# One four-bank PSUM tile for sixteen heads' attention logits, one Exp over it, and reordered first loads, in a four-layer kernel

## The chip, the core and the metric

The kernel runs on one core of a Trainium2 chip. Its engines are TensorE (PE; weight loads are shown apart as PEld), VectorE (DVE), ScalarE (ACT), GpSimd (POOL) and SyncE (SP, which here only issues DMAs). The metric is the device time of one execution in microseconds (us), the median of several runs; less is better. The profile is a hardware trace of one execution.

## The reference

Four layers in a row, each added to its input: attention (A), gated mixer (B), A, B, with the same weights both times. S = 2048 tokens, D = 576, 32 heads of 18 elements. Attention looks back over 8 keys, two tokens apart:

```python
def _A_ref(x, wqkv, wo):                  # H=32, Dh=18, W=8, dil=2
    qkv = (x @ wqkv).reshape(B, S, 3, H, Dh)            # -> q, k, v per head
    idx = pos[:, None] - off[None, :]     # off = 0, 2, ..., 14
    mask = idx >= 0
    kg = k[:, :, idx_c, :]; vg = v[:, :, idx_c, :]      # gathered keys and values
    logits = einsum('bhsd,bhswd->bhsw', q, kg) * Dh ** -0.5
    logits = where(mask, logits, -1e9)
    o = einsum('bhsw,bhswd->bhsd', softmax(logits), vg)
    return o.reshape(B, S, D) @ wo

def _B_ref(x, w_in, w_sp, b_sp, w_out):   # F = 4608, Fh = 2304
    z = gelu(x @ w_in); z1 = z[..., :Fh]; z2 = layernorm(z[..., Fh:])
    g = einsum('ts,bsf->btf', w_sp, z2) + b_sp[None, :, None]
    return (z1 * g) @ w_out

x = x + A(layernorm(x)); x = x + B(layernorm(x))
x = x + A(layernorm(x)); x = x + B(layernorm(x))
```

## The kernel before

All matmul operands are bf16. Each A layer projects q and k in column blocks (`PG`, 512 tokens and 128 columns at a time, for q and k), copies them to a staging tile, and moves them by DMA to one place per head: tile `QK` holds four heads in each group of 128 partitions, 32 partitions a head, of which 18 hold the head and 14 hold fixed window rows. These rows add a large negative number to every logit outside the window, so that a dense 128-key by 112-query product with a plain Exp computes the windowed softmax. The window rows come from a small pattern built on GpSimd and VectorE, written to DRAM (`win_period`) and loaded again (`win_pat`).

The attention loop then runs over 19 token tiles t of 112 queries, twice each for 16 heads (step s, 38 in a layer): logits `L_mm`, Exp `EXP`, values `PV` with the row sums in an extra column of ones. The logits of step s+1 are issued ahead of the values of step s; further work of the layer (late projections `PG`, values `VW`, output projection `WO`, layer norm) is hung into the steps by a table.

```python
def H_tile(self, name):                    # 2 PSUM banks, two of them
    return self.ps.tile([P, 2, 512], f32, name=name, tag="H", bufs=2)
def PT_tile(self, shape, dt, name):        # 1 PSUM bank, four of them
    return self.ps.tile(shape, dt, name=name, tag="PT", bufs=4)
...
def L_mm(s):
    t, hf = divmod(s, 2)
    nk, nq = tdim(t)
    L_tiles[s] = [self.H_tile("L_ps") for _ in range(2)]
    for jp in range(2):
        for ftl in range(4):
            g = 4 * hf + ftl
            for jj in range(2):
                j = 2 * jp + jj            # the group of 32 rows
                nc.tensor.matmul(L_tiles[s][jp][:nk, jj, ftl * QT:ftl * QT + nq],   # line 426
                                 lhsT=kT[32 * j:32 * j + 32, g, QT * t:QT * t + nk],
                                 rhs=qT[32 * j:32 * j + 32, g, QT * t + PADL:QT * t + PADL + nq],
                                 start=True, stop=True, tile_position=(32 * j, 0))
def EXP(s):                                # line 435, two instructions a step
    for jp, L_ps in enumerate(L_tiles.pop(s)):
        Lv = L_ps[:, :, 0:4 * QT].rearrange("p a (b c) -> p a b c", c=QT)
        nc.scalar.activation(out=P_bufs[(2 * s + jp) % 4][:nk, :, :, 0:nq], in_=Lv[:nk, :, :, 0:nq],
                             func=ACT.Exp, scale=scale)
...
L_mm(0); EXP(0)
for d, qk, cc in pre:                      # six more projections
    PG(d, qk, cc, True, q2)
for s in range(NST):
    if s + 1 < NST:
        L_mm(s + 1); EXP(s + 1)
    PV(s)
    for f, a in table.pop(s, []):
        f(*a)
```

The start of the first layer (cut): the first loads go out on two queues, the normalised x of tiles 0 to 3 is transposed on TensorE (`T_pe`, copied to `xnT` by ScalarE), that of the other tiles by DMA on SyncE's queue (`T_`).

```python
x_load(x0[:, 0:2, :], 0, 2, nc.sync); x_load(x0[:, 2:4, :], 2, 2, nc.sync)
self.load_wv(nc.scalar)
x_load(x1[:, 0:4, :], 4, 4, nc.sync)
self.load_wqk(nc.sync)
self.zero_right(); exp_table()
self.build_window_rows(sb, nc.scalar)      # ends with a DMA from ScalarE's queue: win_period
nc.scalar.copy(out=v_ext[:, :, :, DH:DH + 1], in_=self.ones[...])      # line 517
self.make_ident(); setup_bufs(nc.gpsimd)
x_load(spare, 8, 4, nc.sync)
self.load_pat(nc.sync)                     # win_pat <- win_period
for _ in range(28):                        # warming matmuls, result unused
    nc.tensor.matmul(warm[:, 0:P], lhsT=self.ident[:], rhs=self.ident[:], start=True, stop=True)
S_(0, 1); E_(0, 2); R_(0, 2); S_(2); A_(0, 1); T_pe(0); T_pe(1)   # statistics, power on GpSimd, normalise
VW(0, ...); VW(1, ...); ...; T_pe(2); T_pe(3); ...; VW(2, ...)
... A_(4, 5); T_(4, 5); ... A_(6, 7); T_(6, 7)
self.fill_window_rows(QK, 0)
for k_, (d, cc) in enumerate(order):       # (0..2, block 0), (0..2, block 1), (3, 0), (3, 1), (4, 0), (4, 1)
    for qk in ((1, 0) if d < 4 else (0,)):
        PG(d, qk, cc, False, (nc.gpsimd, nc.sync) if d in (0, 4) else (nc.gpsimd, nc.gpsimd, nc.sync))
    if k_ == 3: R_(8, 4); A_(8, 9, 10, 11); T_(8, 9, 10, 11); S_(12, 13, 14, 15); E_(12, 4)
    if k_ == 5: self.fill_window_rows(QK, 1); R_(12, 4); A_(12, 13, 14, 15)
T_(12, 13, 14, 15)
for t in range(3, 8): VW(t, ...)           # then the loop above
```

The last argument of `PG` is the list of queues over which its eight moves into `QK` are dealt in turn. The mixer layers use the same H tiles for their first product and the same PT tiles for the gate and the output.

Of the kernel before, what the change touches and what calls it, by code (L numbers as in the profile page):

```python
# [9 lines left out]
ACT = mybir.ActivationFunctionType  # L10
# [8 lines left out]
P = 128  # L19
# [43 lines left out]
class K:  # L63
# [24 lines left out]
    def setup(self):  # L88
        nc, tc, cfg, ctx = self.nc, self.tc, self.cfg, self.ctx
        S = cfg.S  # L90
        self.consts = ctx.enter_context(tc.tile_pool(name="consts", bufs=1))
        self.dram = ctx.enter_context(tc.tile_pool(name="dram", bufs=1, space=DRAM))
        c = self.consts
        self.neg_half = c.tile([P, 1], f32, name="neg_half")
        nc.vector.memset(self.neg_half[:], -0.5)
        self.eps_t = c.tile([P, 1], f32, name="eps_t")
        nc.vector.memset(self.eps_t[:], EPS)
        self.xnT = c.tile([P, 5, cfg.XW], bf16, name="xnT")
        nc.gpsimd.memset(self.xnT[:, :, 0:PADL], 0.0)

        self.ident = c.tile([P, P], bf16, name="ident")
        self.ones = c.tile([P, 1], bf16, name="ones")
        nc.vector.memset(self.ones[:], 1.0)
        nl = len(cfg.layers)
        self.xres = [self.dram.tile([S, D], f32, name=f"xres{i}") for i in range(nl - 1)]
        self.ps = ctx.enter_context(tc.tile_pool(name="ps", bufs=1, space=PSUM))
        self.right = None
        self.bridge = ctx.enter_context(tc.tile_pool(name="bridge", bufs=1))
        xb = self.bridge.tile([P, 4 * 640], bf16, name="ln_xn")
        self.bsp = xb[:, 0:cfg.S]  # L110
        self.xn_bufs = [xb[:, i * 640:(i + 1) * 640] for i in range(4)]
        self.xn_rr = 0
        self.deferred = []

    def build_window_rows(self, c, eng):
# [31 lines left out]
        nc.vector.tensor_scalar(out=n[:], in0=n[:], scalar1=15, scalar2=None, op0=ALU.bitwise_and)  # L147
        nc.vector.tensor_scalar(out=g[:], in0=n[:], scalar1=1, scalar2=None, op0=ALU.logical_shift_right)
        nc.vector.tensor_tensor(out=g[:], in0=g[:], in1=n[:], op=ALU.bitwise_xor)
        for i in range(4):  # L150
            nc.vector.tensor_scalar(out=bits[:, i, :], in0=g[:], scalar1=i, scalar2=1,
                                    op0=ALU.logical_shift_right, op1=ALU.bitwise_and)
        nc.vector.tensor_scalar(out=bits[:, 4, :], in0=n[:], scalar1=1, scalar2=None, op0=ALU.bitwise_and)
        nc.vector.tensor_scalar(out=vf[:], in0=bits[:], scalar1=-2.0, scalar2=1.0, op0=ALU.mult, op1=ALU.add)
        nc.vector.tensor_scalar_mul(out=R[:, :, 0:8, :], in0=R[:, :, 0:8, :], scalar1=vf[:, 4, 1:2])
        nc.vector.tensor_tensor(out=uu[:], in0=vf[:, 0:4, 0:2], in1=vf[:, 0:4, 1:3], op=ALU.add)
        nc.vector.tensor_scalar_mul(out=R[:, 0, 8:12, :], in0=vf[:, 0:4, 1:2].to_broadcast([P, 4, 16]), scalar1=half)
        nc.vector.tensor_scalar_mul(out=R[:, 1, 8:12, 0:2], in0=uu[:, :, 0:1].to_broadcast([P, 4, 2]), scalar1=0.5)
        nc.vector.tensor_scalar_mul(out=R[:, 1, 8:12, 2:16], in0=uu[:, :, 1:2].to_broadcast([P, 4, 14]), scalar1=0.5)
        one = self.dram.tile([2, MR, 256], bf16, name="win_period")  # L160
# [5 lines left out]
        self.dma(one[:].rearrange("a r (p f) -> p (a r) f", f=16), R[0:16].rearrange("p a r f -> p (a r) f"), eng=eng)  # L166
# [4 lines left out]
        self.load_pat = load  # L171

    def make_ident(self):
        nc = self.nc
        for xb in self.xn_bufs:
            nc.gpsimd.memset(xb[:, D:640], 0.0)
        nc.gpsimd.memset(self.ident[:], 0.0)
        nc.gpsimd.affine_select(out=self.ident[:], in_=self.ident[:], compare_op=ALU.not_equal, fill=1.0,
                                base=0, pattern=[[-1, P]], channel_multiplier=1)
# [12 lines left out]

    def H_tile(self, name):
        return self.ps.tile([P, 2, 512], f32, name=name, tag="H", bufs=2)
# [118 lines left out]
    def layer_A(self, li):  # L313
# [14 lines left out]
        P_bufs = [main.tile([P, 2, 4, P], bf16, name=f"P_sb{k_}") for k_ in range(4)]  # L328
# [9 lines left out]
        if li == 0:  # L338
            w2 = R["win2a"][:].rearrange("p c n -> p (c n)")
            lent = [w2[:, k_ * 2 * CBW:(k_ + 1) * 2 * CBW].rearrange("p (a b) -> p a b", a=2) for k_ in range(2)]  # L340
        man = tc.manual_schedule(engines={ET.PE, ET.Activation, ET.DVE, ET.Pool, ET.SP})
# [73 lines left out]
        L_tiles = {}  # L415

        def L_mm(s):
            t, hf = divmod(s, 2)
            nk, nq = tdim(t)
            L_tiles[s] = [self.H_tile("L_ps") for _ in range(2)]  # L420
            for jp in range(2):
                for ftl in range(4):
                    g = 4 * hf + ftl
                    for jj in range(2):
                        j = 2 * jp + jj
                        nc.tensor.matmul(L_tiles[s][jp][:nk, jj, ftl * QT:ftl * QT + nq],  # L426
                                         lhsT=kT[32 * j:32 * j + 32, g, QT * t:QT * t + nk],
                                         rhs=qT[32 * j:32 * j + 32, g, QT * t + PADL:QT * t + PADL + nq],
                                         start=True, stop=True, tile_position=(32 * j, 0))

        def EXP(s):
            nk, nq = tdim(s // 2)
            for jp, L_ps in enumerate(L_tiles.pop(s)):
                Lv = L_ps[:, :, 0:4 * QT].rearrange("p a (b c) -> p a b c", c=QT)
                nc.scalar.activation(out=P_bufs[(2 * s + jp) % 4][:nk, :, :, 0:nq], in_=Lv[:nk, :, :, 0:nq], func=ACT.Exp,  # L435
                                     scale=scale)

        def PV(s):
            t, hf = divmod(s, 2)
            nk, nq = tdim(t)  # L440
            O_ps = self.PT_tile([P, 512], f32, "O_ps")
            for jp in range(2):
                for ftl in range(4):
                    for jj in range(2):
                        idx = 4 * ftl + 2 * jp + jj
                        nc.tensor.matmul(O_ps[:, idx * (DH + 1):(idx + 1) * (DH + 1)],  # L446
                                         lhsT=P_bufs[(2 * s + jp) % 4][:nk, jj, ftl, :],
                                         rhs=v_ext[:nk, t, 16 * hf + idx, :], start=True, stop=True)
            Ov = O_ps[:, 0:16 * (DH + 1)].rearrange("p (h e) -> p h e", e=DH + 1)
            o_t = o_bufs[t % len(o_bufs)]  # L450
            rec = sb.tile([P, 16], f32, name="rec", tag="rec", bufs=2)
            nc.vector.reciprocal(out=rec[:nq, :], in_=Ov[:nq, :, DH])
            nc.vector.tensor_tensor(out=o_t[:nq, 288 * hf:288 * (hf + 1)].rearrange("p (h d) -> p h d", d=DH),
                                    in0=Ov[:nq, :, 0:DH], in1=rec[:nq, :, None].to_broadcast([nq, 16, DH]), op=ALU.mult)
            if hf == 1:
                c0 = (QT * t) % (RING * P)
                if t < NT - 2:
                    nc.sync.dma_start_transpose(out=oT[:, :, c0:c0 + nq], in_=o_t[:nq, :])
# [38 lines left out]


        if li == 0:
# [11 lines left out]
            self.load_wv(nc.scalar)  # L511
            x_load(x1[:, 0:4, :], 4, 4, nc.sync)
            self.load_wqk(nc.sync)
            self.zero_right()
            exp_table()
            self.build_window_rows(sb, nc.scalar)
            nc.scalar.copy(out=v_ext[:, :, :, DH:DH + 1], in_=self.ones[:, None, None, :].to_broadcast([P, NT, H, 1]))
            self.make_ident()
            setup_bufs(nc.gpsimd)
            x_load(spare, 8, 4, nc.sync)  # L520
            self.load_pat(nc.sync)
            warm = self.PT_tile([P, 512], f32, "warm")
            for _ in range(28):
                nc.tensor.matmul(warm[:, 0:P], lhsT=self.ident[:], rhs=self.ident[:], start=True, stop=True)
# [39 lines left out]
            S_(2)  # L564
# [5 lines left out]
            S_(3)  # L570
            E_(2, 2)
            R_(2, 2)
            VW(1, 0, False)
            VW(1, 1, False)
            S_(4)
# [3 lines left out]
            S_(5)  # L579
# [17 lines left out]
            for k_, (d, cc) in enumerate(order):  # L597
                for qk in ((1, 0) if d < 4 else (0,)):
                    PG(d, qk, cc, False, (nc.gpsimd, nc.sync) if d in (0, 4) else (nc.gpsimd, nc.gpsimd, nc.sync))
# [6 lines left out]
                if k_ == 5:  # L606
                    self.fill_window_rows(QK, 1)
                    R_(12, 4)
                    A_(12, 13, 14, 15)
            T_(12, 13, 14, 15)  # L610
            nvw0, nvw = 3, 8
# [14 lines left out]
        q2 = (nc.gpsimd, nc.sync, nc.gpsimd)  # L626
# [65 lines left out]
    def layer_B(self, li):  # L692
# [7 lines left out]

        zu_cm = pool("zu")
# [257 lines left out]
def build_kernel(ctx, tc, aps, cfg):  # L959
# [7 lines left out]
    k.run_deferred()  # L967

# [53 lines left out]
```

The softmax here doesn't subtract the row's maximum and nothing guards it: scores larger than these inputs give would overflow.

## Time and profile before

| | |
|---|---|
| median time, 3 runs | 1202.52 us (1201.88 to 1202.58) |
| span of the profiled execution | 1199.5 us, 20636 instructions |
| granted TensorE clock, mean | 0.999 |
| attention layers | about 0 to 145 us and 610 to 731 us |
| logits (line 426) | 1216 matmuls 32x112, median 208 ns each |
| Exp (line 435) | 152 instructions, 126.7 us, mean 916 ns for the full shape 128x896 |
| values (line 446) | 1216 matmuls 128x19, median 171 ns each |
| first v projection starts | 12.22 us |
| first q and k projection starts | 18.47 us |

In the profile's views each row is a group of equal instructions in order of time: start, length, engine, line of the kernel, operation, output <- inputs, shape, count, and in brackets the idle time of the engine before it and what ended it. "ACTq", "SPq" are the queues of the engines that issue DMAs. The duration of a matmul runs until its result is written, so that matmuls overlap one another: sixteen of 208 ns can lie within 0.40 us. A weight load may lie beside a matmul.

### The profile page before, as it was taken

To read this page: it belongs to the slowest core of one execution; us is meant where nothing else is said; L and a number is where in the kernel's file an instruction comes from. 1 tells how busy PE (TensorE), PEld (TensorE's weight loads), DVE (VectorE), ACT (ScalarE), POOL (GpSimd) and SP (SyncE) were. 2 spreads that over 40 slices of the span, in tenths; PEclk is the share of its full clock that TensorE was granted. 3 is DMA by queue.
4 is the path that set the end of the run, shared out by engine and by line. 5 is a ranking of instruction groups with operands and counts; after the bars stand their busy time and mean duration, and the time that the engine had idled before them with its cause. 6 is when DMAs were issued, how large, how long until landed. Compare 5 with 4: busy or idle time off the path is not lost.

```text
span 1199.5 us, 20636 instructions
## 1 busy us (share of the span) xinstructions
PE 1173.9 (98%) x8438; PEld 620.1 (52%) x8536; DVE 544.7 (45%) x1199; ACT 377.9 (32%) x599; POOL 273.9 (23%) x381
## 2 busy tenths in 40 slices
PE   7899999999999999999999999999999999999998
PEld 4456644444444444447755675444444444444677
DVE  7577777432332333234555776763323223223311
ACT  4477777301101101101146786770110110111000
POOL 3558874100000000001144777640000000000000
PEclk9999999999999999999999999999999999999999
DMA  6789894000000000049646998900000000000332
GB/s 172 144 176 225 193 207 100 22 1 12 11 11 12 4 8 11 1 136 273 178 91 115 189 235 187 239 1 22 12 11 1 11 11 11 11 1 23 129 104 73
DMA packets 178185, 101.21 MB, mean 84 GB/s; under 512 B 135003, under 2 KB 159435, under 8 KB 178090
## 3 DMA queue, kind: packets, MB, share of 16 engines
q1 hardware_dynamic: 164330, 77.64, 29.5%
q0 software_dynamic: 6480, 15.96, 5.4%
q10 hardware_dynamic: 7280, 6.28, 1.7%
q8 instruction: 67, 1.10, 0.4%
q14 instruction: 28, 0.23, 0.1%
HBM read 42.39 MB, written 16.53 MB: 49 GB/s over the span
## 4 chain that ended last, share of the span: by engine, by line
PE 96%; DMA 2%; issue 1%; ACT 1%; DVE 0%; ACTq 0%; SPq 0%; DVEq 0%
PE pg L856 41%; PE pz L838 12%; PE po L910 12%; PE pz L760 11%; PE pp L391 6%; PE pv L368 4%; PE pw L480 3%; PE O_ps L446 3%; PE L_ps L426 2%; PE pzs L760 1%; ACT P_sb L435 1%; DMA wqk_sb<-in_A_wqkv_dram 1%; DMA QK<-win2a 0%; DMA oT<-o_t 0%; DMA wv_sb<-in_A_wqkv_dram 0%
## 5 line engine op out<-in xcount | busy, mean ns | idle before, releaser
L856 PE MATMUL pg<-Wq,Z 128*128 128x512 bf16 x2256 | 500.3, 379 | 2.5
L856 PEld LDWEIGHTS <-Z 128*128 128x128 bf16 x2304 | 225.2, 98 | 272.0
L860 DVE TENSOR_TENSOR g_tmp<-pg,ln_xn 128x512 f32<-128x512 f32 x144 | 99.6, 692 | 429.2 <-PE pg L856 429.2
L850 ACT ACTIVATE z1T<-pz 128x1024 bf16<-128x1024 f32 x72 | 73.7, 1024 | 513.8 <-PE pz L838 513.6
L77 POOL DMA_DIRECT2D wout<-in_B_w_out_dram x4 | 4.2, 1060 | 604.6 <-PE pg L856 604.6
L910 PE MATMUL po<-wout,Z 128*128 128x288 bf16 x1152 | 141.4, 286 | 0.0
L435 ACT ACTIVATE P_sb<-L_ps 128x896 bf16<-128x896 f32 (+1 forms) x152 | 126.7, 887 | 45.5 <-PE L_ps L426 45.1
L838 PE MATMUL pz<-xnT,w 128*128 128x512 bf16 (+1 forms) x630 | 134.4, 380 | 1.6 <-issue 1.6
L910 PEld LDWEIGHTS <-Z 128*128 128x128 bf16 x1152 | 112.7, 98 | 28.8
L760 PEld LDWEIGHTS <-xnT 128*128 128x128 bf16 (+1 forms) x800 | 66.2, 97 | 81.0 <-issue 23.8
L760 PE MATMUL pz<-win2a,xnT 128*128 128x512 bf16 x366 | 103.5, 380 | 0.8
L861 DVE TENSOR_TENSOR Z<-g_tmp,z1T 128x512 bf16<-128x512 f32 x144 | 99.6, 692 | 9.7
L838 PEld LDWEIGHTS <-w 128*128 128x128 bf16 (+1 forms) x640 | 51.1, 97 | 80.0 <-issue 27.1
L391 PE MATMUL pp<-xnT,wqk_sb 128*128 128x512 bf16 x340 | 81.6, 382 | 4.2 <-DMA xnT<-ln_xn 3.1
L774 ACT ACTIVATE zp<-pz 128x1024 bf16<-128x1024 f32 x64 | 65.5, 1024 | 36.7 <-PE pz L760 33.8
L235 POOL TENSOR_SCALAR ln_xn<-x_new,ln_mv,ln_rstd 128x576 bf16<-128x576 f32 x32 | 73.3, 2292 | 2.8
L920 DVE TENSOR_TENSOR x_new<-po,xo 128x288 f32<-128x288 f32 (+1 forms) x64 | 28.8, 455 | 88.0 <-PE po L910 83.6
L760 PE MATMUL pz<-win2b,xnT 128*128 128x512 bf16 (+1 forms) x256 | 65.8, 380 | 0.0
L776 DVE CUSTOM_DVE_ANT_0 Z<-zp 128x1536 bf16<-128x1536 bf16 x32 | 56.4, 1762 | 15.9 <-ACT zp L774 15.9
L77 POOL DMA_DIRECT2D QK<-stg x81 | 51.6, 641 | 52.3 <-DVE stg L360 32.1
L368 PE MATMUL pv<-wv_sb,xnT 128*128 128x288 bf16 (+1 forms) x380 | 57.0, 290 | 2.9 <-DMA wqk_sb<-in_A_wqkv_dram 2.3
L391 PEld LDWEIGHTS <-wqk_sb 128*128 128x128 bf16 x360 | 33.4, 98 | 39.9 <-issue 4.0
(111 smaller groups left out, 883.8 us busy)
## 6 DMA issues: line engine op xcount, KB each, us to landing
xres<-x_new SPq DMA_DIRECT2D x48, 288.0 KB
xo<-xres SPq DMA_DIRECT2D x48, 288.0 KB
wout<-in_B_w_out_dram POOLq DMA_DIRECT2D x4, 1296.0 KB, 8.1
w<-in_B_w_in_dram SPq DMA_DIRECT2D x16, 256.0 KB
QK<-stg POOLq DMA_DIRECT2D x53, 72.0 KB, 4.4
QK<-stg SPq DMA_DIRECT2D x41, 72.0 KB
xo<-in_A_x_dram SPq DMA_DIRECT2D x16, 144.0 KB
win2a<-in_B_w_in_dram POOLq DMA_DIRECT2D x6, 288.0 KB, 4.2
```

Of the source, the lines that this page charges most:

```text
L235: e.tensor_scalar(out=xn[:nrows, 0:D], in0=x_t[:nrows, :], scalar1=mv[:nrows, 0:1], scalar2=rstd[:nrows, 0:1], op0=ALU.subtract, op1=ALU.mult)
L368: nc.tensor.matmul(pv[:nk, 0:288], lhsT=self.xnT[:, c, QT * t:QT * t + nk], rhs=wv_sb[:, c, hh * 288:(hh + 1) * 288], start=(c == 0), stop ...
L391: nc.tensor.matmul(pp[:, :], lhsT=w, rhs=self.xnT[:, c, PADL + cc * 512:PADL + (cc + 1) * 512], start=(c == 0), stop=(c == 4))
L435: nc.scalar.activation(out=P_bufs[(2 * s + jp) % 4][:nk, :, :, 0:nq], in_=Lv[:nk, :, :, 0:nq], func=ACT.Exp, scale=scale)
L760: nc.tensor.matmul(pzvs[ci][:, sub * 512:sub * 512 + w], lhsT=self.xnT[r0:r1, c, PADL + i * P:PADL + (i + 1) * P], rhs=win2(c)[r0:r1, c0 + ...
L774: nc.scalar.activation(out=zp[:, c0:c0 + cn], in_=pzvs[ci][:, 0:cn], func=ACT.Gelu_apprx_tanh, accum_out=sums[:, ci:ci + 1])
L838: nc.tensor.matmul(pz1s[q // 2][:, q % 2, :], lhsT=w1[r0:r1, c, sub * P:(sub + 1) * P], rhs=self.xnT[r0:r1, c, PADL + q * 512:PADL + (q + ...
L850: nc.scalar.activation(out=z1T[:, q2 * 512:(q2 + 2) * 512], in_=pz1s[q2 // 2][:, :, :].rearrange("p a b -> p (a b)"), func=ACT.Gelu_apprx_ ...
L856: nc.tensor.matmul(pg[:, :], lhsT=Z[:, jj, i, sub * P:(sub + 1) * P], rhs=Wq[q][:, i, :], start=(i == 0), stop=(i == NS - 1))
L860: nc.vector.tensor_tensor(out=tmp[:], in0=pg[:, :], in1=bsp[:, qs], op=ALU.add)
L861: nc.vector.tensor_tensor(out=uT(jj)[:, sub, qs], in0=tmp[:], in1=z1Ts[jj, sub][:, qs], op=ALU.mult)
L910: nc.tensor.matmul(acc[hh], lhsT=uT(j // 2)[:, j % 2, i * P:(i + 1) * P], rhs=wouts[j // NJH][:, j % NJH, hh * 288:(hh + 1) * 288], start= ...
```

## The change

Logits: the two H tiles of a step become one tile of four banks, one bank for each group of 32 rows; the sixteen matmuls go round the four groups in turn, and one Exp of 128x1792 takes the place of two of 128x896. The P buffers become two of double size. As the four-bank tile needs the room of both H tiles, that pool is opened anew for every layer. The aim is fewer instructions on ScalarE and four row groups at work at once.

Start: the first loads go out on SyncE's queue in order of need (x of tiles 0 to 3, weights of v, x of tiles 4 to 7, weights of q and k, more x). The identity is built first and 46 instead of 28 warming matmuls follow it. The window rows' VectorE work is cut in two parts laid between the statistics, and their DMA moves later in ScalarE's program. The values of token tile 3 are computed between two projection blocks, the normalisation of tiles 12 to 15 goes ahead of a large VectorE fill, and the moves of the last column block (d = 4) all go out from GpSimd, so that SyncE is free sooner for the transposes.

The diff, with the body of the window rows' helper cut:

```diff
+    def open_H(self, name):
+        if self.hp_cm is not None:
+            self.hp_cm.__exit__(None, None, None)
+        self.hp_cm = self.tc.tile_pool(name=name, bufs=1, space=PSUM, reuse_waits="tile")
+        self.hp = self.hp_cm.__enter__()
+
     def H_tile(self, name):
-        return self.ps.tile([P, 2, 512], f32, name=name, tag="H", bufs=2)
+        return self.hp.tile([P, 2, 512], f32, name=name, tag="H", bufs=2)
...
-        P_bufs = [main.tile([P, 2, 4, P], bf16, name=f"P_sb{k_}") for k_ in range(4)]
+        P_bufs = [main.tile([P, 4, 4, P], bf16, name=f"P_sb{k_}") for k_ in range(2)]
...
+        self.open_H(f"A{li}_H")
+        Hs = self.hp.tile([P, 4, 512], f32, name="L_ps")
...
         def L_mm(s):
             t, hf = divmod(s, 2)
             nk, nq = tdim(t)
-            L_tiles[s] = [self.H_tile("L_ps") for _ in range(2)]
-            for jp in range(2):
-                for ftl in range(4):
-                    g = 4 * hf + ftl
-                    for jj in range(2):
-                        j = 2 * jp + jj
-                        nc.tensor.matmul(L_tiles[s][jp][:nk, jj, ftl * QT:ftl * QT + nq],
...
+            for ftl in range(4):
+                g = 4 * hf + ftl
+                for j in range(4):
+                    nc.tensor.matmul(Hs[:nk, j, ftl * QT:ftl * QT + nq],
+                                     lhsT=kT[32 * j:32 * j + 32, g, QT * t:QT * t + nk],
+                                     rhs=qT[32 * j:32 * j + 32, g, QT * t + PADL:QT * t + PADL + nq],
+                                     start=True, stop=True, tile_position=(32 * j, 0))
 
         def EXP(s):
             nk, nq = tdim(s // 2)
-            for jp, L_ps in enumerate(L_tiles.pop(s)):
-                Lv = L_ps[:, :, 0:4 * QT].rearrange("p a (b c) -> p a b c", c=QT)
-                nc.scalar.activation(out=P_bufs[(2 * s + jp) % 4][:nk, :, :, 0:nq], in_=Lv[:nk, :, :, 0:nq], func=ACT.Exp,
-                                     scale=scale)
+            Lv = Hs[:, :, 0:4 * QT].rearrange("p a (b c) -> p a b c", c=QT)
+            nc.scalar.activation(out=P_bufs[s % 2][:nk, :, :, 0:nq], in_=Lv[:nk, :, :, 0:nq], func=ACT.Exp, scale=scale)
...
+        q2 = (nc.gpsimd, nc.sync, nc.gpsimd)
...
-            self.load_wv(nc.scalar)
+            self.load_wv(nc.sync)
             x_load(x1[:, 0:4, :], 4, 4, nc.sync)
             self.load_wqk(nc.sync)
+            x_load(spare, 8, 4, nc.sync)
+            exp_table()
             self.zero_right()
-            exp_table()
-            self.build_window_rows(sb, nc.scalar)
+            self.make_ident()
+            warm = self.PT_tile([P, 512], f32, "warm")
+            for _ in range(46):
+                nc.tensor.matmul(warm[:, 0:P], lhsT=self.ident[:], rhs=self.ident[:], start=True, stop=True)
+            rows = self.build_window_rows(sb)
             nc.scalar.copy(out=v_ext[:, :, :, DH:DH + 1], in_=self.ones[:, None, None, :].to_broadcast([P, NT, H, 1]))
-            self.make_ident()
             setup_bufs(nc.gpsimd)
-            x_load(spare, 8, 4, nc.sync)
-            self.load_pat(nc.sync)
-            warm = self.PT_tile([P, 512], f32, "warm")
-            for _ in range(28):
-                nc.tensor.matmul(warm[:, 0:P], lhsT=self.ident[:], rhs=self.ident[:], start=True, stop=True)
...
-            S_(2)
+            rows[0]()
             A_(0, 1)
             T_pe(0)
             T_pe(1)
             VW(0, 0, False)
             VW(0, 1, False)
-            S_(3)
+            S_(2, 3)
             E_(2, 2)
             R_(2, 2)
+            rows[1](nc.scalar)
+            self.load_pat(nc.sync)
             VW(1, 0, False)
             VW(1, 1, False)
-            S_(4)
             A_(2, 3)
...
-                    PG(d, qk, cc, False, (nc.gpsimd, nc.sync) if d in (0, 4) else (nc.gpsimd, nc.gpsimd, nc.sync))
+                    PG(d, qk, cc, False, ((nc.gpsimd, nc.sync), q2, q2, q2, (nc.gpsimd,))[d])
+                if k_ == 2:
+                    VW(3, 0, False)
+                    VW(3, 1, False)
...
                 if k_ == 5:
-                    self.fill_window_rows(QK, 1)
                     R_(12, 4)
                     A_(12, 13, 14, 15)
+                    self.fill_window_rows(QK, 1)
             T_(12, 13, 14, 15)
-            nvw0, nvw = 3, 8
+            nvw0, nvw = 4, 8
```

## The prediction

> **What bounds the kernel now.** I read the page from the top: the engines' busy shares, then the chain that ended last.
>
> ```profile
> PE 1173.9 (98%) x8438; PEld 620.1 (52%) x8536; DVE 544.7 (45%) x1199; ACT 377.9 (32%) x599; POOL 273.9 (23%) x381
> ...
> PE 96%; DMA 2%; issue 1%; ACT 1%; DVE 0%; ACTq 0%; SPq 0%; DVEq 0%
> ```
>
> TensorE is the bound: 96% of the chain, and only 1199.5 - 1173.9 = 25.6 us of the span without a matmul in flight. The change touches neither mixer layer's matmuls, so all it can move lies in the two attention stages, about 0 to 145 us and 610 to 731 us. The list of waits gives the idle pieces of TensorE:
>
> ```profile
> PE warm L524 <- POOL ident L178: 5.7, 1, 5.7
> PE pp L391 <- DMA xnT<-ln_xn: 3.1, 1, 3.1
> PE pv L368 <- DMA wqk_sb<-in_A_wqkv_dram: 2.3, 1, 2.3
> PE L_ps L426 <- ACT P_sb L435: 2.2, 6, 0.4
> ```
>
> Columns: who waited, for whom, us in total, times, longest. The first three belong to the start of the first layer. The last is the wait that the new PSUM tile touches: in 76 steps the logits wait for the Exp only 2.2 us in all. The TensorE timeline in the second attention layer shows how one step of its loop lies:
>
> ```profile
> 674.58 0.40 PE L426 MATMUL L_ps<-QK 32*128 32x112 bf16 x16
> 674.90 0.56 PE L446 MATMUL O_ps<-v_ext,P_sb 128*128 128x19 bf16 x16
> 675.32 0.77 PE L368 MATMUL pv<-wv_sb,xnT 128*128 128x288 bf16 x5
> 675.93 0.78 PE L480 MATMUL pw<-wo_sb,oT 128*128 128x288 bf16 x5
> 676.64 0.56 PE L426 MATMUL L_ps<-QK 32*128 32x112 bf16 x16
> ```
>
> and the ScalarE timeline beside it:
>
> ```profile
> 675.05 1.73 ACT L435 ACTIVATE P_sb<-L_ps 128x896 bf16<-128x896 f32 x2 [0.58 <-PE L_ps L426]
> 676.66 0.41 ACT L362 CAST v_ext<-pv 128x288 bf16<-128x288 f32 x1
> 677.11 1.73 ACT L435 ACTIVATE P_sb<-L_ps 128x896 bf16<-128x896 f32 x2
> ```
>
> What is to be seen: the sixteen logit matmuls take 0.40 us in one step and 0.56 us in the next. They are short when both H tiles are free at their start; then all four row groups run side by side already, although the code issues them in pairs. They are long where the second tile comes free only when the previous step's second Exp ends (675.05 + 1.73 = 676.78). Steps start at 674.58, 676.64, 678.86, 680.92: 2.06 and 2.22 us in turn, 2.14 on average. ScalarE works 1.73 + 0.41 of each, so it is nearly as full as TensorE here.
>
> **What the Trainium skill says.** "TensorEngine Tiling (Array Packing)", Key Properties: tiles of different row groups work independently. The trace agrees (0.40 us with four groups in play, 0.56 us with two and two). "TensorE: Matmul & The Clock Gate", Part 1: TensorE falls to half clock after a window with too little work and returns after a busy one. The trace agrees: after the 3.1 us wait the table of windows gives a granted clock of 0.50 for 56 to 59 us. "ScalarE: Activation LUTs", What ACT_TABLE_LOAD costs: a fixed part plus 0.833 ns per element. The trace has 916 ns for 896 elements and 1024 ns for 1024, so 0.844 ns per element. "SBUF — State Buffer", Who interferes with whom and the section above it: a VectorE copy can hold off GpSimd through their shared port. The trace fits: the small GpSimd power takes 2.18 us beside the large VectorE fills at 39.72, 1.05 us at 30.85.
>
> **The change part by part: the loop.** Two Exps of 916 ns become one of 916 + 896 x 0.844 = 1672 ns; back to back the two took 1.73 us, so ScalarE saves 0.06 us a step, about 4 us of busy time over 76 steps, off the path. Against it stands the buffering. Before, two H tiles let the first half of the next logits be written while the second Exp ran, and ScalarE could go from Exp to Exp. Now one tile holds all four banks: the next logits wait for the whole Exp, and the next Exp for all sixteen matmuls. This makes a ring: start of logits to start of Exp 675.05 - 674.58 = 0.47 us; Exp 1.67; end of Exp to the next matmul 0.05 (Exps at 105.58 + 1.73 = 107.31, the waiting half of the logits at 107.36). Sum 2.19, say 2.2 us as the least step. The 0.16 us of a slow logit group is not won back as such: those groups were slow because they waited for the same Exp.
>
> Steps longer than 2.2 us (those with query and key projections inside, 2.5 to 3.1 us) don't change. Shorter ones grow to 2.2. From 674.58 to 715.06 there are 19 steps, 40.5 us; at 2.2 they need 41.8: +1.3. From 643.04 to 655.00 six steps take 12.0; at 2.2 13.2: +1.2, of which some 0.4 returns because the next step waits inside before (its logits stand in two pieces at 655.00 and 655.75). The first layer looks alike (58.27 to 70.14 and 86 to 131 us), so I take +2.0 a layer, **+4.0 us** together.
>
> **The start.** The first v projections (line 368) begin at 12.22. The wait list names a weight load, but on ScalarE's timeline the copy of the transposed x begins only at 11.15, behind a copy of ones that ran 8.81 to 11.63 (2.82 us), itself behind the window-row transfer that ScalarE's queue issued at 8.42. The change moves that transfer later, so the ones copy can run at about 3.4 and end at 6.2. GpSimd's own list of small work still ends at about 6.5, then the power (0.73), the normalisation (0.72 for two tiles), transposes and a 0.7 us copy: first v matmul at about 9.5. The weights for v, now fourth in one queue behind 4 tiles of x, land by about 6 to 7. The 46 warming matmuls start near 1.6 instead of 5.71, so the clock should be full by then; before, 20 v matmuls took 3.94 us, later ten take 1.23. Query and key projections start near 14.5 instead of 18.47.
>
> That lead is not kept whole. The second column block needs four transposes by DMA, issued 16.25 to 22.47 behind the window-pattern loads, which wait for the window-row transfer; I leave them where they are, plus 1.5 us from issue to use (54.53 to 56.04 before): 24.0. Before, that block began at 18.47 + 6 x 1.08 = 24.95. So 0.95 us, plus the v matmuls of tile 3 done earlier in the gap (10 x 0.123 = 1.2): first logits at 41.9 instead of 44.12.
>
> Next, SyncE's queue. It issued seven late QK moves from 43.00 to 49.23 and then the last transposes to 54.53; TensorE waited for these until 56.04 and then ran at half clock to 58.27. The change gives all eight moves of the last column block to GpSimd: 4 x 0.89 = 3.6 us less on SyncE, 1.0 from the lead. The transposes land by about 51.4, and the 3.1 us wait and the half-clock 1.1 us go. But GpSimd, which ended at 46.76, gets 4 x 0.57 = 2.3 us more, less the 1.0: its last issue is near 47.0, and 4.4 us from issue to landing (page, part 6) is the pessimistic bound. The second logits, wanted at 48.9, then wait until 50.5 to 51.5. After them come the last two early projections (2.2 us): the third logits start at about 53.5 instead of 58.27: **-4.8 us**.
>
> **Sum:** 1202.5 - 4.8 + 4.0 = 1201.7; I take 1201.5, as some of the ring's cost should hide in the loop's other waits.
>
> **Rivals.** (1) Interleaving really shortens every logit group: 0.1 to 0.16 us in 76 steps, 8 to 12 us, to about 1188. For it speaks that half of the groups show 0.56; against it, that these are the ones next to a late Exp, and that paired issue already reaches 0.40. (2) The ring costs more: if the single Exp starts 0.1 us later or evacuations come between, 50 short steps lose 5 us more: 1206.5. For it: ScalarE's 0.41 us casts lie between the Exps; against: they fit in the 0.5 us in which ScalarE waits for logits. (3) The lead at the start is wholly hidden because GpSimd's QK moves end last: then only the transposes' wait and the half clock are won in part, 2 us, and the kernel lands at 1202.5 - 2 + 4 = 1204.5. (4) The start keeps its lead of 4 us as well as the 4.2: 1202.5 - 8.2 + 4 = 1198.3.
>
> **Range and chances.** The start is worth 2 to 8 us, the loop costs 1 to 6; they do not lean on each other. So 1196 to 1206, predicted 1201.5. Two per cent is 24 us; it would need rival 1 twice over or a stall I do not see: 0.03 faster, 0.95 within, 0.02 slower.
>
> **What would show it.** Exps of 128x1792 at about 1.67 us, 72 of them; logits starting about 2.2 us apart in the light steps, with 0.40 us everywhere; in the list of waits, logits waiting for Exp at well over 2.2 us in total; first v matmul near 9.5 and projections near 14.5, a wait for DMA transposes at about 22 to 24; no wait for them and no half clock near 56; the third logits near 53.5. The prediction is wrong if light steps stay at 2.06 (the ring is shorter than I sum it), or if the start's lead is gone by the third logits.

## The result: 0.66% slower, and the profile after

The changed kernel takes 1209.81 us (median of 4 runs, 1207.34 to 1213.01) against 1202.2 us before: a ratio of 1.0066, 95% interval 1.0039 to 1.0092. That is within 2%, but outside the predicted 1196 to 1206. The profiled execution of after has a span of 1205.6 us and a mean granted clock of 0.996; before it was 1199.5 us and 0.999.

The page of after, with the engines' busy shares, the chain that ended last, and the one row of Exp (line, engine, operation, tiles, shapes, count, then busy us, mean ns, idle us before it):

```profile
PE 1171.6 (97%) x8456; PEld 619.0 (51%) x8554; DVE 544.9 (45%) x1197; ACT 373.5 (31%) x523; POOL 276.7 (23%) x383
PE 87%; ACT 7%; DMA 2%; issue 1%; DVE 1%; POOL 1%; SPq 0%; ACTq 0%; DVEq 0%
L442 ACT ACTIVATE P_sb<-L_ps 128x1792 bf16<-128x1792 f32 (+1 forms) x76 | 122.1, 1607 | 55.6 <-PE L_ps L434 55.6
```

ScalarE does 76 instructions and 4.4 us less work. But it has entered the chain: 7% where it had 1%, since TensorE now waits for the Exp and the Exp for TensorE. The span grew by 6.1 us while TensorE's busy time fell by 2.3 us (1173.9 to 1171.6): TensorE is not busy for longer, it waits longer. The list of waits of TensorE names what for (us in total, times, longest):

```profile
PE L_ps L434 <- ACT P_sb L442: 8.7, 21, 1.3
PE pp L403 <- DMA xnT<-ln_xn: 3.1, 1, 3.1
PE L_ps L434 <- DMA QK<-win2a: 2.7, 1, 2.7
PE warm L524 <- POOL ident L182: 1.5, 1, 1.5
PE L_ps L434 <- DMA QK<-stg: 1.0, 1, 1.0
```

The first row was 2.2 us before. The wait for the identity fell from 5.7 to 1.5, as intended. The two rows of logits waiting for DMAs into `QK` are new: 3.6 us that the prediction did not have at this place.

The loop, on TensorE's and on ScalarE's timeline of after, in the same second attention layer as before:

```profile
683.64 0.38 PE L434 MATMUL L_ps<-QK 32*128 32x112 bf16 x16
685.84 0.38 PE L434 MATMUL L_ps<-QK 32*128 32x112 bf16 x16
```

```profile
684.12 1.66 ACT L442 ACTIVATE P_sb<-L_ps 128x1792 bf16<-128x1792 f32 x1 [0.54 <-PE L_ps L434]
685.68 0.40 ACT L374 CAST v_ext<-pv 128x288 bf16<-128x288 f32 x1
```

In this stretch every logit group takes 0.38 us, none 0.56, and every step 2.20 us; these are light steps, without q and k projections inside. The ring can be read off: 684.12 - 683.64 = 0.48 from logits to Exp, 1.66 of Exp (ending at 685.78), 0.06 to the next logits at 685.84. That the pool of the tile is opened anew for every layer costs nothing: from the last values of the first attention layer to the first of the second it is 501.9 us, against 501.8 before.

The start, on TensorE's timeline of after:

```profile
24.68 14.80 PE L403 MATMUL pp<-xnT,wqk_sb 128*128 128x512 bf16 x59 [3.06 <-DMA xnT<-ln_xn]
...
44.31 0.28 PE L434 MATMUL L_ps<-QK 32*128 32x112 bf16 x8
47.26 0.23 PE L434 MATMUL L_ps<-QK 32*128 32x112 bf16 x3 [2.67 <-DMA QK<-win2a]
48.45 0.34 PE L434 MATMUL L_ps<-QK 32*128 32x112 bf16 x5 [0.97 <-DMA QK<-stg]
48.80 8.32 PE L403 MATMUL pp<-xnT,wqk_sb 128*128 128x512 bf16 x29
...
59.28 0.38 PE L434 MATMUL L_ps<-QK 32*128 32x112 bf16 x16 [0.27 <-ACT P_sb L442]
```

The first group of logits stands in three pieces. The third group (59.28) comes 1.0 us later than before (58.27) although the first v matmul came 3.4 us earlier (8.77 against 12.22). The table of windows shows why the projections stretch (columns: window, its length, busy us of TensorE, weight loads, VectorE, ScalarE and GpSimd, then granted clock, DMA share, GB/s):

```profile
20.00:30.00 10.00, 6.88 (x28) 3.10 (x28) 7.73 (x17) 2.76 (x6) 0.62 (x1) 0.83 0.51 109
50.00:60.00 10.00, 9.68 (x95) 4.56 (x95) 7.39 (x11) 2.44 (x3) 2.52 (x3) 0.87 0.82 155
70.00:80.00 10.00, 8.17 (x147) 4.83 (x149) 5.32 (x12) 6.49 (x5) 3.47 (x6) 0.83 0.86 201
```

A granted clock of 0.83 over 10 us is half clock for about 3.4 us (10 x 0.17 / 0.5). Before, this happened once in the first 150 us, between 50 and 60. After has three such stretches, the second split over 40 to 60.

The starts of the values (`PV`) tell where the 6.1 us of this execution arose: those of step 1 come 0.8 us later than before, those of step 37, the last of the first layer, 3.9 later, and in the second layer the lag grows by another 2.1. So most of it arises in the loops, though the first loop also holds the half-clock stretch at 70 to 80 us and a wait of 1.8 us for the transposed attention output (`oT`).

### The profile page after: what moved, and what is told of

It reads as the page before. It is cut to its first block, busy times and chain, and to the rows that moved or that the text cites. A ratio compares the mean times of both kernels' runs of the same rounds, so it can differ in the third digit from the quotient of the medians.

```text
span 1205.6 us, 20519 instructions
## 1 busy us (share of the span) xinstructions
PE 1171.6 (97%) x8456; PEld 619.0 (51%) x8554; DVE 544.9 (45%) x1197; ACT 373.5 (31%) x523; POOL 276.7 (23%) x383
## 4 chain that ended last, share of the span: by engine, by line
PE 87%; ACT 7%; DMA 2%; issue 1%; DVE 1%; POOL 1%; SPq 0%; ACTq 0%; DVEq 0%
PE pg L865 41%; PE pz L847 12%; PE po L919 12%; PE pz L769 11%; ACT P_sb L442 7%; PE pp L403 4%; PE L_ps L434 2%; PE pw L482 2%; PE pzs L769 1%; DMA QK<-stg 1%; PE pv L380 1%; PE O_ps L449 1%; POOL QK L77 1%; DMA win_period<-win_rows 0%; DMA oT<-o_t 0%
## 5 line engine op out<-in xcount | busy, mean ns | idle before, releaser
L442 ACT ACTIVATE P_sb<-L_ps 128x1792 bf16<-128x1792 f32 (+1 forms) x76 | 122.1, 1607 | 55.6 <-PE L_ps L434 55.6
L403 PE MATMUL pp<-xnT,wqk_sb 128*128 128x512 bf16 x340 | 85.1, 394 | 4.2 <-DMA xnT<-ln_xn 3.1
```

The costliest lines, as they stand in the source:

```text
L403: nc.tensor.matmul(pp[:, :], lhsT=w, rhs=self.xnT[:, c, PADL + cc * 512:PADL + (cc + 1) * 512], start=(c == 0), stop=(c == 4))
L442: nc.scalar.activation(out=P_bufs[s % 2][:nk, :, :, 0:nq], in_=Lv[:nk, :, :, 0:nq], func=ACT.Exp, scale=scale)
```

## The experiments

Two theories stood after the result. **Ring:** the single tile and single Exp make the least step 2.2 us. **Start:** the new order at the start brings TensorE's work forward, but not the transfers it needs. The rival to both was that the order of matmuls, or the clock alone, did it. All ratios are to the kernel before, measured on the same chip in the same turn, with 95% intervals.

### The start alone and the loop alone

`start_only` is after with the loop of before:

```diff
-        Hs = self.hp.tile([P, 4, 512], f32, name="L_ps")
+        L_tiles[s] = [self.H_tile("L_ps") for _ in range(2)]   # pairs, two Exps, four P buffers: as before
```

> The start of the changed kernel (load order, warming matmuls, moved row work, queue of the last moves) with the logits of the kernel before: two H tiles of two banks, pairs of row groups, two Exps a step. Theory R (the one tile makes a ring of logits and Exp with a least step of 2.2 us, and that is where the loss is): the loops return to 2.14 us a light step, so the time is that of before plus what the start gave in the trace of the changed kernel (third logits at 59.28 against 58.27, so +1): 1203 us, interval of the ratio within 0.999 to 1.003. Theory S (the rearranged start is the loss, with its waits and half-clock windows): 1206 to 1210.

Measured: 1206.03 us (13 runs), ratio 1.0026 [1.0016, 1.0035], so +3.1 us. The start, meant to gain, loses by itself. TensorE's timeline of `start_only` at the first logits:

```profile
42.70 0.27 PE L436 MATMUL L_ps<-QK 32*128 32x112 bf16 x4
45.29 0.34 PE L436 MATMUL L_ps<-QK 32*128 32x112 bf16 x9 [2.32 <-DMA QK<-stg]
46.98 0.22 PE L436 MATMUL L_ps<-QK 32*128 32x112 bf16 x1 [1.35 <-DMA QK<-stg]
48.55 0.28 PE L436 MATMUL L_ps<-QK 32*128 32x112 bf16 x2 [1.35 <-DMA QK<-stg]
```

TensorE arrives at 42.70, 1.4 us ahead of before, and then waits three times, 5.0 us in all, for moves into `QK`. The timeline of SyncE's queue in this run shows where those moves stood:

```profile
32.20 7.06 SPq L252 DMA_TRANSPOSE xnT<-ln_xn  x4
39.35 5.06 SPq L77 DMA_DIRECT2D QK<-stg  x5
```

The four transposes of tiles 8 to 11 take the queue for 7 us, and five moves that the logits read are issued behind them, until 44.41. The same stretch before:

```profile
32.39 6.14 SPq L242 DMA_TRANSPOSE xnT<-ln_xn  x4
38.63 4.27 SPq L77 DMA_DIRECT2D QK<-stg  x5
...
44.12 0.49 PE L426 MATMUL L_ps<-QK 32*128 32x112 bf16 x16
```

The order on the queue is the same before. The issue is 0.7 us later in `start_only` (39.35 against 38.63), but the last piece of the logits stands 4.4 us later (48.55 against 44.12): the moves also took longer to land. This execution of `start_only` was the slowest of the thirteen (1209.37 us). It is 8.0 us longer than the profiled execution of before (1207.5 against 1199.5): 1.7 stand at the values of step 1, and 4.6 more arise by step 25 of the first loop, though that is the old loop: it holds a wait of 2.7 us for `oT` and half clock at 70 to 80 and at 100 to 110 us.

`loop_only` is before with the four-bank tile, the order round the four groups and the single Exp:

```diff
-            L_tiles[s] = [self.H_tile("L_ps") for _ in range(2)]
+        Hs = self.hp.tile([P, 4, 512], f32, name="L_ps")       # one tile, one Exp, two P buffers: as after
```

> The logits of the changed kernel (one four-bank tile, four groups in turn, one Exp) with the start of the kernel before. Theory R: +2 us in each attention layer and little more, 1206 to 1208; light steps 2.20 us apart in the trace. Theory S: within 1 us of before.

Measured: 1206.78 us (7 runs), ratio 1.0032 [1.0020, 1.0045], so +3.9 us. The two halves add up to the whole: 0.26% + 0.32% = 0.58% against 0.66%, well within the intervals. In its trace the light steps start 2.20 us apart and logits wait for Exp 8.7 us in 20 waits. The values of the second layer's last step come 2.1 us later against those of its first step than before, at full clock. Over the whole kernel the clock has a part in the +3.9: its mean was 0.9953 in these runs and 0.9971 in the 19 of before.

### The order of the matmuls without the big tile

`inter_two` keeps two tiles and two Exps and changes only the order:

```diff
-            for jp in range(2):
-                for ftl in range(4):
-                    g = 4 * hf + ftl
+            for ftl in range(4):
+                g = 4 * hf + ftl
+                for jp in range(2):
```

> The kernel before with one edit: the sixteen logit matmuls go round the four row groups in turn, still into two H tiles and with two Exps. Theory R: the order itself gains nothing, since paired issue reached 0.40 us already; the first matmul of the second tile now stands third and waits for the second Exp of the step before, so the first Exp starts later: +1 to +3 us, 1203 to 1205. Rival I (interleaving saves the 0.16 us of the slow groups): 1196 to 1200.

Measured: 1207.23 us (6 runs), ratio 1.0042 [1.0030, 1.0054], +5 us; more than expected. TensorE's timeline of `inter_two`:

```profile
683.60 0.55 PE L426 MATMUL L_ps<-QK 32*128 32x112 bf16 x16
685.82 0.54 PE L426 MATMUL L_ps<-QK 32*128 32x112 bf16 x16
688.03 0.55 PE L426 MATMUL L_ps<-QK 32*128 32x112 bf16 x16
```

No group is short any more, and these steps take 2.21 us instead of 2.06 and 2.22 in turn; the second layer loses 2.4 us. In the new order the third matmul already writes the second tile, which the previous step's second Exp still holds (on ScalarE's timeline the two Exps end at 684.21 + 1.73 = 685.94, after the logits' start at 685.82); so the first tile is not filled early and the first Exp cannot start early. Interleaving bought nothing here: 0.38 us against 0.40 for a paired group that does not wait.

### The Exp's length

`loop_halfexp2` is `loop_only` with an Exp over half of the columns. The other half of P is set to ones once, so half of the softmax is left out; the matmuls are the same.

```diff
-            nc.scalar.activation(out=P_bufs[s % 2][:nk, :, :, 0:nq], in_=Lv[:nk, :, :, 0:nq], ...)
+            nc.scalar.activation(out=P_bufs[s % 2][:nk, :, 0:2, 0:nq], in_=Lv[:nk, :, 0:2, 0:nq], ...)
```

> As loop_only, but each Exp covers only two of the four column groups, 128x896 of 128x1792 elements, and the rest of P holds ones: half of the Exp is left out. Theory R: the ring shrinks to 0.48 + 0.91 + 0.05 = 1.45 us, below the matmuls' own work, so light steps fall to 2.04 to 2.06 us and logits hardly wait for an Exp; the profile then shows what TensorE alone would take, some 1196 to 1200. If the wait were for anything but the Exp's length, the steps would stay at 2.20.

Measured, in a single run: 1201.38 us, above the 1196 to 1200 that were expected; TensorE waits 6.9 us for `oT` in it (1.7 before). What the run is for stands in its light steps. TensorE's timeline, and ScalarE's beside it:

```profile
683.33 0.38 PE L431 MATMUL L_ps<-QK 32*128 32x112 bf16 x16
685.37 0.38 PE L431 MATMUL L_ps<-QK 32*128 32x112 bf16 x16
```

```profile
683.82 0.92 ACT L439 ACTIVATE P_sb<-L_ps 128x896 bf16<-128x896 f32 x1 [1.12 <-PE L_ps L431]
```

The same tile and the same sixteen matmuls step in 2.04 us once the Exp is 0.92 us long, and the second attention layer is 2.3 us shorter than before. So the Exp's length sets the 2.20 us. The remaining 2.04 is TensorE's own work: its groups follow one another there without a listed wait.

### What holds the start up

`start_q` gives the moves the queues of before, and puts the large VectorE fill ahead of the last normalisation again:

```diff
-                    PG(d, qk, cc, False, ((nc.gpsimd, nc.sync), q2, q2, q2, (nc.gpsimd,))[d])
+                    PG(d, qk, cc, False, (nc.gpsimd, nc.sync) if d in (0, 4) else (nc.gpsimd, nc.gpsimd, nc.sync))
...
                 if k_ == 5:
+                    self.fill_window_rows(QK, 1)
                     R_(12, 4)
                     A_(12, 13, 14, 15)
-                    self.fill_window_rows(QK, 1)
```

> start_only with two of its edits undone: the queues over which the moves of the column blocks go out, and the order of the large VectorE fill ahead of the last normalisation, are as in the kernel before. Theory Q (GpSimd issues the third and fourth column block's moves earlier now and these get ahead of the moves that the first logits need): the first logits' wait of 5.0 us falls to 1 to 2 us, third logits at about 56, 1203 to 1204. Theory D (the moves behind SyncE's four transposes are late for the same reason as before, the transposes themselves): the wait stays at 4 to 5 us, 1206.

`start_T` keeps the new queues, moves the fill likewise, and issues the transposes of tiles 8 to 11 behind the moves of block d = 2:

```diff
                 if k_ == 3:
                     R_(8, 4)
                     A_(8, 9, 10, 11)
-                    T_(8, 9, 10, 11)
...
                 if k_ == 5:
+                    T_(8, 9, 10, 11)
+                    self.fill_window_rows(QK, 1)
                     R_(12, 4)
                     A_(12, 13, 14, 15)
-                    self.fill_window_rows(QK, 1)
```

> start_only with the four DMA transposes of tiles 8 to 11, which nothing needs before the first logits, put behind the moves of the first three column blocks on SyncE's queue, and the large fill ahead of the last normalisation as before. Theory D: first logits wait under 1.5 us, starting at 42.7; the gain can come back as a wait for the transposes in the early projections behind them. 1201 to 1204. Theory Q: the wait stays above 3 us.

`start_fill` is `start_only` with 13 and 20 unused matmuls, where TensorE waited for the second block and for the first logits:

```diff
+                    for _ in range(13):                        # after VW(3); 20 more ahead of L_mm(0)
+                        nc.tensor.matmul(fill[:, :], lhsT=self.ident[:], rhs=self.xnT[:, 0, 0:512], start=True, stop=True)
```

> start_only with 13 matmuls of 512 columns, results unused, in the wait for the transposes at 21.7 us and 20 ahead of the first logits: they add no work that anything waits for. Theory H (the rest of the start's loss is TensorE at half clock after these idle pieces): no half clock between 20 and 57 us, 1.5 to 3 us less than start_only, 1203 to 1204.5. If half clock matters little, within 1 us of start_only (1206).

| kernel | us (runs) | ratio to before | first logits wait for moves |
|---|---|---|---|
| start_only | 1206.03 (13) | 1.0026 [1.0016, 1.0035] | 5.0 us |
| start_q | 1204.27 (13) | 1.0007 [0.9993, 1.0021] | 0.3 us |
| start_T | 1203.78 (21) | 1.0005 [0.9995, 1.0015] | 0.3 us |
| start_fill | 1205.38 (13) | 1.0015 [1.0005, 1.0024] | 1.2 us, the rest filled |

Both reorderings take the wait away, and with it the difference from before. They don't gain. Nor do they tell which edit did it. In `start_q` the moves still stand behind the same four transposes; SyncE's queue and TensorE's timeline:

```profile
32.10 6.42 SPq L252 DMA_TRANSPOSE xnT<-ln_xn  x4
38.61 4.26 SPq L77 DMA_DIRECT2D QK<-stg  x5
...
43.19 0.96 PE L436 MATMUL L_ps<-QK 32*128 32x112 bf16 x11 [0.28 <-DMA QK<-stg]
```

So standing behind the transposes does not by itself make the wait, as theory D had it (4 to 5 us); and `start_T`, with the new queues, has none, against theory Q (above 3 us). How long a move takes to land differs: for the 72 KB moves that GpSimd issued at 36 to 48 us from the staging tile, a median of 7.2 us from issue in `start_only`, 5.0 in `start_q`, 5.2 before. And the two runs share an edit: both put the VectorE fill ahead again. With it GpSimd's power takes 2.18 us instead of 1.04, and GpSimd's next moves start at 41.32 and 41.46 instead of 39.71, that is later against those that the first logits need. No run has this edit alone, so whether the queues, the transposes or the fill made the moves late stays open.

In `start_q` waits come back elsewhere (`xnT` by DMA, 6.4 us in two waits, 3.1 in one before). In `start_T` the third logits do come early, and the lead is then lost. From its TensorE timeline:

```profile
45.25 8.32 PE L401 MATMUL pp<-xnT,wqk_sb 128*128 128x512 bf16 x30 [2.10 <-DMA xnT<-ln_xn]
...
98.06 1.38 PE L490 MATMUL pw<-wo_sb,oT 128*128 128x288 bf16 x5 [2.79 <-DMA oT<-o_t]
```

The values of step 1 lie 2.56 us ahead of before, those of step 17 still 0.9 ahead, those of step 18 1.5 behind: between them stands a wait of 2.79 us for the transposed attention output (1.2 us before), and the five output matmuls behind it take 1.38 us instead of 0.77 because the clock is halved again.

`start_fill` tells the clock's part. Its windows have no half clock from 20 to 60 us, where `start_only` had 0.83 over 40 to 60 (its row stands last):

```profile
20.00:40.00 20.00, 19.25 (x101) 9.61 (x99) 13.40 (x34) 9.20 (x18) 10.70 (x17) 1.00 0.71 132
40.00:60.00 20.00, 18.84 (x167) 9.87 (x165) 12.44 (x19) 7.55 (x13) 9.48 (x14) 1.00 0.92 145
...
40.00:60.00 20.00, 14.70 (x110) 7.22 (x113) 10.83 (x16) 5.61 (x10) 9.40 (x13) 0.83 0.89 132
```

The two profiled executions are the fastest of thirteen and the slowest of thirteen, so they do not measure the difference. The means over all runs point the same way: the clock was 0.9937 in `start_only` against 0.9971 in the 19 runs of before beside it, and 0.9965 in `start_fill` against 0.9962 in 41. By the ratios filling the waits gives back 0.11% or 1.3 us of the 3.1, though the intervals of 1.0026 and 1.0015 overlap; what is left, 0.15%, is not a matter of the mean clock.

### Could the lead be kept?

A last theory was that the DMA engines are a second bound at 70 to 100 us, and that six loads of mixer weights (288 KB each, steps 5 to 15 of the first loop) delay `oT`. The edit spreads them over steps 8 to 28. `before_late` makes it in before, `T_late` in `start_T`, and `T_late_fill` adds 7 and 10 unused matmuls to `T_late`:

```diff
-                at(5 + 2 * k_, f)
+                at(8 + 4 * k_, f)
```

> The kernel before with one edit: the six 288 KB loads of the mixer's weights (win2a), hung into steps 5, 7, ... 15 of the first attention loop, go into steps 8, 12, ... 28 instead. Theory D (in steps 5 to 20 the DMA engines are the second bound, so that a lead won at the start is lost there): before has a 1.2 us wait for oT and long DMA shares at 70 to 120 us, so 0.5 to 2 us come back, 1200.5 to 1202 us. Rival (only the half clock and the start decide; the loads are hidden whenever they go): within 0.3 us of before.

> The kernel start_T (the change's start with the transposes of tiles 8 to 11 moved behind the moves of the block d = 2) with the same edit of the weight loads. Theory D: the 2.8 us wait for oT at 98 us shrinks to under 1 us, with it the half clock beside it, and of the lead of 2.6 us at the third logits 1.5 to 2.5 us stays: 1200 to 1201.5 us, faster than before by 0.1 to 0.2%. Rival: the wait for oT comes from SyncE's order alone; it stays at 2 to 3 us and the time at 1203 to 1204.5.

> T_late with 7 unused 512-column matmuls ahead of the second column block and 10 behind the first logits, where TensorE waits for DMA transposes. If half-clock windows after those waits cost time (start_fill), the clock stays full from 20 to 60 us and another 0.5 to 1.5 us come back against T_late: 1199 to 1200.5 us. If the windows only follow load later on, the same as T_late within 0.5 us.

Measured: `before_late` 1203.68 us, 1.0005 [0.9993, 1.0016]; `T_late` 1208.94 us, 1.0047 [1.0029, 1.0064]; `T_late_fill` 1205.23 us, 1.0022 [1.0009, 1.0034]. No gain in any, and `T_late` is slower. Its TensorE timeline:

```profile
96.74 0.79 PE L490 MATMUL pw<-wo_sb,oT 128*128 128x288 bf16 x5 [0.89 <-DMA oT<-o_t]
...
116.19 0.79 PE L490 MATMUL pw<-wo_sb,oT 128*128 128x288 bf16 x5 [1.86 <-DMA oT<-o_t]
```

The wait near 97 us fell from 2.79 to 0.89 as expected. A wait of 1.86 us came at 116 us, and half clock over 110 to 130 us behind it. The lead of 1.0 us at step 25 was a lag of 2.3 at step 32. So in this execution the wait went when the loads moved, and another came. That the load on the DMA engines makes these waits is not shown: over 100 to 120 us their share was 1.12 here, and 1.24 before, where TensorE waits only 0.5 us for `oT` in that stretch. This was the fastest of the eight runs; why `T_late` loses more in the others was not settled; its mean clock is 0.9925 over 8 runs against 0.9966 in the 37 of before. No version that beats before was found.

## Why the prediction was wrong

**The loop: right in its mechanism.** The ring was summed as 0.47 + 1.67 + 0.05 = 2.2 us and measured as 0.48 + 1.66 + 0.06 = 2.20. The Exp was taken as 1672 ns and is 1663 (median). +2.0 us a layer was predicted; the second layer shows +2.1, `loop_only` as a whole +3.9 against +4.0; that this is so near is in part luck, since the clock differed too. In the first layer of that trace the loop lost 4.7 us (from 0.8 ahead at step 1 to 3.9 behind at step 37), but a half clock at 110 to 120 us is in it, so its ring alone can't be read there; in the trace of after the first loop lost 3.0 us. `inter_two` and `loop_halfexp2` show the mechanism: with two tiles the order costs as much, and with a short Exp the ring does not bind. Rival 1 (interleaving shortens every group) falls. The prediction also read 0.40 and 0.56 us as four groups at work and two and two; `inter_two` has 0.55 with all four in turn, so the 0.56 shows the wait and not the number of groups.

**The start: wrong, -4.8 predicted, +3.1 measured alone.** Most of its early steps held: first v matmul 8.77 (predicted 9.5), first projections 13.76 (14.5), second block at 24.68 after a wait for DMA transposes (24.0). No wait for the last transposes follows, as predicted. The step that failed is "first logits at 41.9". It added up TensorE's work and took for granted that the moves into `QK` would have landed. At that point I followed only the queues that had made TensorE wait before, the late moves and the last transposes. Before, SyncE had issued its staged moves by 42.90 (38.63 + 4.27) and the logits began at 44.12 without a wait; in `start_only` TensorE is there at 42.70, and the last of the moves that it needs has landed only at 48.55, 5.0 us of waiting in three pieces (3.6 in two in after). Why they landed so late stays open, as said above. This is what rival 3 had in view (the lead hidden by QK moves that end last), only one logit group earlier and on SyncE's queue as well. The 50.5 to 51.5 us wait foreseen for the second group did not come: in after that group begins at 57.05 without a wait. Its sum was off as well (46.76 + 2.3 - 1.0 is 48.1, not 47.0 for GpSimd's last issue), which had no effect.

The second thing missing is "no half clock near 56". One half-clock stretch did go; others came. The 59 projections of the second block take 14.80 us in after and 13.11 in `start_only` at full clock: 1.7 us for one stretch. Summed up to the third logits in after: block two 0.7 late, half clock 1.7, the moves 3.6, half clock again 8.32 - 6.63 = 1.7, less some 2 us for the wait that did not come. That is 5.7, of the 59.28 - 53.5 = 5.8 us that are missing there. The range shared the fault: it gave the start 2 to 8 us of gain and left no room for a loss.

The third thing is that a lead at 53 us was taken for a lead at the end. `start_T` had 2.56 us of it at step 1 and was 2.0 behind at the end of the first loop; a wait for `oT` and half clock stand in between. Adding start and loop was sound within the intervals; the sign of the start was wrong. A start at +3.1 puts my own sum at 1202.5 + 3.1 + 4.0 = 1209.6.

## What to carry to other kernels

A step that an engine reaches earlier is only earlier if every transfer it reads lands earlier as well: follow each operand to its DMA, to what stands ahead of it in that queue and to how long such transfers took to land, not only those that were waited for before. Merging two buffers into one bigger tile trades an instruction's fixed cost (here 126.7 - 122.1 = 4.6 us of ScalarE's time over 76 steps, 0.06 us a step) for a ring of producer and consumer; sum the ring first and compare it with the step as it is. Go through the waits behind a lead before counting it as won.

## What the runs showed of the hardware that was not expected

Half clock came after waits of TensorE shorter than the stretch itself: behind 2.10 us of waiting in `start_T` (45.25) the 30 projections took 8.32 us instead of 6.63 (`start_q`, 44.16). "TensorE: Matmul & The Clock Gate", Part 1, says that the windows run freely at about 3.4 us, and that the count of slow matmuls differs from run to run. The traces agree with the length (3.4 us by the windows of after) and with the variation. It puts the penalty of the ramp under 1% of a typical kernel and advises not to fit a count of slow matmuls; here the whole effect of the change is 0.66%, so stretches of half clock later in the kernel cannot be left out of the account. In the four runs of after the time goes from 1207.34 to 1213.01 us as the mean clock goes from 0.996 to 0.990, close to 1 us for each thousandth (the 13 runs of `start_only` give 0.6 by a straight line).

Issuing on another queue did not make transfers independent. "DMA: Bandwidth & Descriptors", Issuing engines are not separate DMA queues, says that all of them end on the same 16 engines. The trace fits: in `start_only` four transposes took 7.06 us of SyncE's queue (6.14 before) while GpSimd's moves went out faster beside them (ten in 5.95 us against eleven in 7.84). That this contention made them slower is an inference; no run varied it alone.
